# Keys and values of the next batch made in the unused columns of the score tiles

## The chip, the cores and the metric

The kernel runs on one core of a Trainium2 chip. The metric is device time in microseconds (us), the median of three runs. The names of the engines are those of the profile: PE (TensorE, with its weight loads as PEld), DVE (VectorE), ACT (ScalarE), POOL (GpSimd) and SP (SyncE, which issues the DMAs here).

## What is computed

An attention over pooled keys, and behind it a feed-forward layer with a SoLU activation and a layer norm. Four batches of 12288 queries, 768 keys each, width 128, hidden width 1024:

```python
kv_pool = kv.reshape(B, H // r, r, W // r, r, C).mean(axis=(2, 4))
kv_flat = kv_pool.reshape(B, -1, C) @ w_sr
k = v = kv_flat
s = scale * (q @ k.transpose(0, 2, 1))
a = np.exp(s - s.max(-1, keepdims=True))
a /= a.sum(-1, keepdims=True) + 1e-09
x = (a @ v).reshape(B * S, C)
h = x @ w_in
e = np.exp(h - np.max(h, axis=-1, keepdims=True))
solu = h * (e / (np.sum(e, axis=-1, keepdims=True) + 1e-09))
ln = (solu - mean(solu)) / np.sqrt(var(solu) + 1e-06) * g_ln
out = ln @ w_out
```

## The kernel before, in words

The rows of all batches are cut into 384 tiles of 128 queries, 96 tiles to a batch; four tiles are a group. One loop runs over 384 slots. A slot works on several tiles at once, each in another stage, so the engines are a pipeline, and the order in which the loop writes its calls is the order in which each engine works: nothing is rescheduled (`tc.manual_schedule`). In slot t:

- PE makes the scores of tile t+1 (`scores_pe`, L386): six matmuls into a PSUM tile `s` of two banks, 2 x 512 float32 columns, of which 2 x 384 are used.
- DVE takes the maximum of a score row (`nm`, L402, for tile t at the head of slot t), ACT the exponent in place (L403) and its rounded high part (`phl`, L407), DVE the low part (the score split, L415). DMA transposes both (`pT`).
- PE multiplies the transposed weights with the values of the batch (`values`, L453): 18 matmuls a group into one PSUM bank `xa`, spread over four slots, the quarters of the group. `values_out` (ACT, `xh`, L459) and `values_split` (DVE, `xl`, L464) read it when a group is done.
- PE makes the hidden row of tile t-9 (`hidden_pe`, `h`, L505, six matmuls), DVE the scaled maximum of tile t-10 (`junkd`, L513), ACT its exponent (`e`, L529), and in the slot behind it DVE the product `u` (L543), ACT the sum of squares (`junk`, L603), POOL the two float16 parts of `u` (`uhl`, L560 and L566). DMA transposes them (`uT`).
- PE makes the output of tile t-13 (`final_pe`, `o`, L631, 24 matmuls), which DVE scales (`ob`, L674).

The score tiles `s` and the hidden tiles `h` share three PSUM buffers in turn (`ps_r`). So the hidden product of slot t starts when DVE's split of tile t has read its score tile, and the scores of slot t start when `u` of tile t-11 has read its hidden tile.

On DVE a slot runs: hidden maximum, score split, (in one slot of four the reciprocal `rz`, L487, and half of `ob`; in another the other half), score maximum of the next tile, `u`, (in one slot of four `xl`). On ACT: `e`, (in one slot of four `xh`; in another a small `rz` and the rounding of the next queries `qh`), score exponent, `phl`, `junk`, then the next `e`.

Keys and values of batch b+1 are made beside batch b by a table `PLAN` of slots (counted within batch b). Its sum over the 16 pooled rows lies in `ka`. PE multiplies it with the weights (`kv_k_pe`, L235, in slots 69 and 73, one half of 384 keys each) and ACT copies the product to `ks` (L238). From `ks` come the rounded parts: `kv_kh` (ACT, L241, slots 72 and 76), `kv_sq` (ACT, a sum of squares, L260, slots 75 and 77), `kv_kl` and `kv_kc` (POOL). In slots 85 and 89 PE transposes `ks` (`kv_v_pe`, L286, three blocks a half) and ACT copies the result with a scale to `vf` (L291). Both kinds of product go to the bank of `xa`, in the one slot of a group in which the values of the last group are read and those of the next not yet begun; in these four slots the values of the first quarter (three matmuls instead of four) are written behind the hidden and the final product (`late`, `with_keys`). ACT's copy stands behind `e` of its slot. All this happens three times (batch 0's own keys are made ahead of the loop): in slots 69 to 91, 165 to 187 and 261 to 283.

Of the kernel before, what the change touches and what calls it, by code (L numbers as in the profile page):

```python
# [17 lines left out]
AF = mybir.ActivationFunctionType  # L18
# [4 lines left out]
B = 4  # L23
# [6 lines left out]
TPB = NTOK // P  # L30
WARM = 14
NT = B * TPB
GT = 4
GPB = TPB // GT
NG = NT // GT
# [9 lines left out]
LAV = 2  # L45
# [32 lines left out]
def kernel(  # L78
# [15 lines left out]
    nc = tc.nc  # L94
# [47 lines left out]
    state = {}  # L142
# [17 lines left out]
    def half_of(name, b, half):  # L160
        return state[name, b][:, half * 384 : half * 384 + 384]
# [67 lines left out]
    def kv_psum(b, name):  # L229
        pool, tag = (ps_x, "x") if b or name == "pv_0_0" else (ps_o, "o")  # L230
        return pool.tile([P, 512], F32, tag=tag, name=name)

    def kv_k_pe(b, half):
        state["pk", half] = kv_psum(b, f"pk_{b}_{half}")
        nc.tensor.matmul(state["pk", half][:, :384], w_sr16, half_of("ka", b, half), start=True, stop=True)  # L235

    def kv_k_out(b, half):
        nc.scalar.copy(half_of("ks", b, half), state.pop(("pk", half))[:, :384])  # L238

    def kv_kh(b, half):  # L240
        nc.scalar.copy(half_of("kh", b, half), half_of("ks", b, half))  # L241
# [125 lines left out]
    def scores_pe(t):  # L367
        g, j = divmod(t, GT)
        b = t // TPB
        qh, ql = state["q", g]  # L370
        qt = state["qf", g // QL].bitcast(BF16).rearrange("p (n two) -> p n two", two=2)[:, :, 1]
        kh, kl, kc = (state[n, b] for n in ("kh", "kl", "kc"))
        ts = slice(j * P, (j + 1) * P)
        s = ps_r.tile([P, 2, 512], F32, tag="r", name=f"s_{t}")
        if t in PY:
            py = s[:, 0, 384:385]
            for half in range(2):
                nc.tensor.matmul(
                    py, onesm, state["kss", PY[t]][:, half : half + 1], start=half == 0, stop=half == 1
                )  # L380
            state["py", PY[t]] = py
        row = [(n, half, *x) for n, x in enumerate(((ql, kc), (qh, kh), (qt, kl))) for half in range(2)]
        if t == 0:
            row = sorted(row[2:4] + row[:2] + row[4:], key=lambda x: x[1])
        for n, half, lh, rh in row:
            nc.tensor.matmul(  # L386
                s[:, half, :384],
                lh[:, ts],
                rh[:, half * 384 : (half + 1) * 384],
                start=n == (t == 0),  # L390
                stop=n == 2,
            )
        state["s", t] = s[:, :, :384]

    def scores_exp(t, between=()):

        g, j = divmod(t, GT)
        if j == 0:
            state["z", g] = tiny.tile([P, GT], F32, tag="z", name=f"z_{g}", bufs=4)
        s = state["s", t]  # L400
        nm = tiny.tile([P, 1], F32, tag="nm", name=f"nm_{t}", bufs=3)
        nc.vector.tensor_reduce(nm, s, axis=AX.XY, op=ALU.max, negate=True)  # L402
        nc.scalar.activation(s, s, AF.Exp, bias=nm, accum_out=state["z", g][:, j : j + 1])  # L403
        for f in between:
            f()
        phl = dmt.tile([P, 2, 2, 384], F16, tag="phl", name=f"phl_{t}", bufs=4)
        nc.scalar.mul(phl[:, 0], s, SC)  # L407
        state["phl", t] = phl
# [15 lines left out]
        )  # L424


    def with_keys(g):


        b, ti = divmod(GT * g + GT - 1 + LAV, TPB)  # L430
        return g > 1 and b + 1 < B and ti in WITH_PE

    def values(g, qtr, part):
        share = {0: [0, 6, 6, 6], 1: [0, 6, 6, 6]}.get(g, [4, 5, 5, 4])
        if with_keys(g):
            share = [3, 5, 5, 5]
        s0 = sum(share[:qtr])
        s1 = s0 + share[qtr]
        if s0 == s1:
            return  # L440
        cut = s0 + (s0 > 0)
        s0, s1 = ((s0, cut), (cut, s1))[part]
        b = g * GT // TPB
        if s0 == 0 and s1:
            state["xa", g] = ps_x.tile([P, 512], F32, tag="x", name=f"xa_{g}")
        if s0 == s1:
            return
        xa, pT = state["xa", g], state["pT", g]
        vh, vl = state["vh", b], state["vl", b]
        seq = [(a, c, v) for c in range(NKC) for (a, v) in ((0, vh), (1, vh), (0, vl))]  # L450
        for n in range(s0, s1):
            a, c, v = seq[n]
            nc.tensor.matmul(  # L453
                xa, v[:, c, :], pT[:, :, a * NKC + c, :], start=n == 0, stop=n == len(seq) - 1
            )
# [239 lines left out]
    ident = const.tile([P, P], F32, name="ident")  # L695
# [7 lines left out]
    w_sr16 = const.tile([P, P], F32, name="w_sr16")  # L703
# [139 lines left out]
    def w_low():  # L843
# [14 lines left out]


    PLAN = [  # L860
        (69, 0, kv_k_pe, kv_k_out), (73, 1, kv_k_pe, kv_k_out),
        (72, 0, kv_kh), (76, 1, kv_kh),
        (73, 0, kv_kl), (77, 1, kv_kl), (78, 0, kv_kc), (82, 1, kv_kc),
        (75, 0, kv_sq), (77, 1, kv_sq),
        (80, 0, kv_bound), (81, 1, kv_bound), (84, 2, kv_bound),
        (85, 0, kv_v_pe, kv_v_out), (87, 0, kv_v_high), (88, 0, kv_v_low),
        (89, 1, kv_v_pe, kv_v_out), (90, 1, kv_v_high), (91, 1, kv_v_low),
    ]
    WITH_PE = {slot for slot, _, *fs in PLAN if len(fs) > 1}


    def at(t, fn, *args):
        if 0 <= t < NT:
            fn(t, *args)
# [13 lines left out]
    for b in range(1, B):  # L888
        for k, fs in kv_plan(b):
            plan.setdefault((b - 1) * TPB + k, []).append(fs)  # L890
    scores_pe(0)
    for slot in range(NT):
        i = slot - LH
        av, qtr = divmod(slot - LAV - GT + 1, GT)
        tb, ti = divmod(slot, TPB)
# [3 lines left out]
        todo = plan.pop(slot, [])  # L899
# [11 lines left out]
        if 0 <= av < NG:  # L911
            values(av, qtr, 0)
        at(slot + 1, scores_pe)
        at_soon(slot - NORM, values_norm)
        at_last(slot - FSC, final_scale)
# [10 lines left out]
            hidden_var(i - 1)  # L926
        for f in fill.get(slot, []):
            f()
        pairs = [st for st in todo if len(st) > 1 and st[0].func is not kv_add]
        for st in pairs:  # L930
            st[0]()
        late = 0 <= av < NG and qtr == 0 and with_keys(av)
        if 0 <= av < NG and not late:
            values(av, qtr, 1)
        for st in pairs:
            for f in st[1:]:
# [12 lines left out]
        at_last(slot - LO, final_half, 0)  # L949
        if slot < NT - 1:  # L950
            at(slot - LO, final_pe)
        if late:
            values(av, qtr, 1)
        at(i - 1, hidden_turn)
        at_last(slot - LO - 1, final_out)
        at_last(slot - XSP, values_out)
# [18 lines left out]
    def tail_values(g):  # L975
# [5 lines left out]
        h=hidden_pe, M=hidden_max, E=hidden_exp, U=hidden_u, J=hidden_var, hi=hidden_high,  # L981
# [49 lines left out]
```

## Time and profile before

| what | value |
|---|---|
| median of 3 runs | 1853.36 us (1851.58 to 1855.24) |
| profiled execution, first to last instruction (span) | 1847.1 us |
| median of the runs less the span | 6.3 us |
| busy PE, DVE, ACT, POOL | 99%, 97%, 95%, 87% |
| granted TensorE clock | 0.9 or more of full speed in all 40 slices of the page; 1.000 as the mean |
| DMA engines, mean busy share by slice | 0.8 to 0.9 and more |

The page gives the profiled execution its span and no other time; the 6.3 us by which the timed median is longer are taken to lie around it. A busy PE counts each matmul with its modelled tail, and these overlap: what a matmul costs is the time from its start to the next one's. The same holds, by about a tenth of a microsecond, for DVE and ACT.

### The profile page before, as it was taken

The page shows a single profiled execution, that of the slowest core. Times are in us where ns is not written, and L with a number is a line of the kernel's source. Part 1 is how long each engine was busy: PE and PEld are TensorE (multiplying, and loading weights), DVE is VectorE, ACT ScalarE, POOL GpSimd, SP SyncE. Part 2 cuts the span into 40 slices and gives each one's busy share as a digit, 9 for nine tenths or more (in the row PEclk, how much of TensorE's full clock was granted, in tenths as well). Part 3 has the DMA queues.
Part 4 walks back from the last instruction along what each step waited for, and adds up shares of the span by engine and source line. Part 5 has one row for each costly group of instructions (what it writes and reads, how often), then busy time and mean ns, then how long its engine had stood idle before and what let it go on. Part 6 is the DMA issues. An engine that isn't in the chain of part 4 may idle for free.

```text
span 1847.1 us, 43152 instructions
## 1 busy us (share of the span) xinstructions
PE 1821.1 (99%) x15717; PEld 1179.2 (64%) x15718; DVE 1784.9 (97%) x2729; ACT 1752.8 (95%) x3148; POOL 1613.8 (87%) x1392
## 2 busy tenths in 40 slices
PE   8999999999999999999999999999999999999999
PEld 4566666666666666666666666666666666666666
DVE  7999999999999999999999999999999999999998
ACT  6999999999999999999999999999999999999998
POOL 3899889899998999989988899989888888888887
PEclk9999999999999999999999999999999999999999
DMA  8999999999999999999999999999999999999998
GB/s 300 208 238 233 229 245 234 236 240 245 232 234 240 244 238 241 235 233 238 235 233 234 247 241 241 238 236 231 227 217 230 233 228 223 230 227 231 224 223 179
DMA packets 1473253, 431.80 MB, mean 234 GB/s; under 512 B 1400977, under 2 KB 1454353, under 8 KB 1472785
## 3 DMA queue, kind: packets, MB, share of 16 engines
q1 hardware_dynamic: 1472752, 428.98, 114.1%
q8 instruction: 124, 2.03, 0.5%
q14 instruction: 89, 0.72, 0.1%
q10 hardware_dynamic: 288, 0.07, 0.0%
HBM read 52.50 MB, written 25.17 MB: 42 GB/s over the span
## 4 chain that ended last, share of the span: by engine, by line
PE 63%; DVE 13%; ACT 7%; POOL 7%; issue 7%; DMA 3%; DVEq 0%; POOLq 0%; ACTq 0%
PE o L631 19%; PE h L505 18%; PE xa L453 13%; PE s L386 13%; DVE junkd L513 3%; DVE nm L402 3%; POOL uhl L566 3%; DVE phl L415 2%; ACT e L529 2%; DMA pT<-phl 2%; ACT junk L603 2%; POOL uhl L560 2%; ACT phl L407 2%; DVE u L543 1%; DVE ob L674 1%
## 5 line engine op out<-in xcount | busy, mean ns | idle before, releaser
L566 POOL TENSOR_TENSOR uhl<-u,uhl 128x1024 f16<-128x1024 f32 x382 | 815.1, 2134 | 31.7 <-ACT uhl L558 0.2
L631 PEld LDWEIGHTS <-uT 128*128 128x128 f16 x9072 | 537.1, 98 | 91.9 <-DMA uT<-uhl 7.0
L631 PE MATMUL o<-wch,uT 128*128 128x128 f16 x6048 | 568.0, 219 | 1.3 <-DMA uT<-uhl 1.3
L631 PE MATMUL o<-wcl,uT 128*128 128x128 f16 x3024 | 525.9, 219 | 0.0
L560 POOL TENSOR_SCALAR uhl<-u 128x1024 f16<-128x1024 f32 x377 | 393.5, 1044 | 136.2 <-DVE u L543 131.1
L543 DVE SCALAR_TENSOR_TENSOR u<-h,rz,e 128x1024 f32<-128x1024 f32 x384 | 491.2, 1279 | 16.0 <-ACT e L529 3.6
L513 DVE TENSOR_SCALAR_CACHE_REDUCE junkd<-h,rz 128x1024 bf16<-128x1024 f32 x384 | 491.5, 1280 | 1.4 <-PE h L505 1.0
L529 ACT ACTIVATE e<-h,nm,rz 128x1024 f32<-128x1024 f32 x384 | 459.0, 1195 | 1.0 <-DVE junkd L513 1.0
L603 ACT ACTIVATE junk<-u,su 128x1024 bf16<-128x1024 f32 x384 | 437.8, 1140 | 0.2 <-DVE u L543 0.2
L402 DVE TENSOR_REDUCE nm<-s 128x1 f32<-128x768 f32 x384 | 365.7, 952 | 23.3 <-PE s L386 20.8
L453 PE MATMUL xa<-pT,vh 128*128 128x512 f16 x1152 | 373.5, 379 | 6.6 <-DMA pT<-phl 4.0
L403 ACT ACTIVATE s<-s,nm 128x768 f32<-128x768 f32 x384 | 335.9, 875 | 41.9 <-DVE nm L402 37.1
L415 DVE SCALAR_TENSOR_TENSOR phl<-s,phl 128x768 f16<-128x768 f32 x384 | 366.3, 954 | 4.5 <-ACT phl L407 4.3
L407 ACT ACTIVATE phl<-s 128x768 f16<-128x768 f32 x384 | 311.0, 810 | 11.7
L505 PEld LDWEIGHTS <-xh 128*128 128x128 f16 x1536 | 144.8, 97 | 191.7 <-issue 26.7
L386 PE MATMUL s<-kh,qh 128*128 128x384 f32 x768 | 248.0, 404 | 0.1
L505 PE MATMUL h<-w_in_h,xh 128*128 128x512 f16 x768 | 228.2, 379 | 3.5 <-DVE rz L487 2.4
L505 PE MATMUL h<-w_in_h,xl 128*128 128x512 f16 x768 | 228.4, 379 | 0.0
L505 PE MATMUL h<-w_in_l,xh 128*128 128x512 f16 x768 | 228.3, 379 | 0.0
L453 PE MATMUL xa<-pT,vl 128*128 128x512 f16 x576 | 218.3, 379 | 0.0
L386 PE MATMUL s<-kc,ql 128*128 128x384 bf16 x768 | 187.8, 326 | 7.4 <-DVE phl L415 4.4
L386 PE MATMUL s<-kl,qf 128*128 128x384 bf16 x768 | 192.2, 332 | 0.1
(127 smaller groups left out, 1707.2 us busy)
## 6 DMA issues: line engine op xcount, KB each, us to landing
kv<-in_kv_dram SPq DMA_DIRECT2D x64, 384.0 KB, 4.3
qf<-in_q_dram SPq DMA_DIRECT2D x96, 256.0 KB, 3.3
out_dram<-ob SPq DMA_DIRECT2D x95, 256.0 KB, 2.8
pT<-phl SPq DMA_TRANSPOSE x384, 3.8
uT<-uhl SPq DMA_TRANSPOSE x378, 4.4
raw_in<-in_moe_w_in_dram SPq DMA_DIRECT2D x1, 1024.0 KB, 5.4
raw_out<-in_moe_w_out_dram SPq DMA_DIRECT2D x1, 1024.0 KB, 8.6
out_dram<-ob SPq DMA_DIRECT2D x1, 192.0 KB, 2.0
```

Of the source, the lines that this page charges most:

```text
L386: nc.tensor.matmul(s[:, half, :384], lh[:, ts], rh[:, half * 384 : (half + 1) * 384], start=n == (t == 0), stop=n == 2,)
L402: nc.vector.tensor_reduce(nm, s, axis=AX.XY, op=ALU.max, negate=True)
L415: nc.vector.scalar_tensor_tensor(phl[:, 1], state.pop(("s", t)), SC, phl[:, 0], op0=ALU.mult, op1=ALU.subtract)
L453: nc.tensor.matmul(xa, v[:, c, :], pT[:, :, a * NKC + c, :], start=n == 0, stop=n == len(seq) - 1)
L505: nc.tensor.matmul(h[:, hs], lh[:, ts], rh[:, hs], start=n == 0, stop=n == 2)
L513: nc.vector.tensor_scalar(junk, state["h", t], state["rz", g][1][:, j : j + 1], None, op0=ALU.mult, op1=ALU.min, accum_out=nm,)
L529: nc.scalar.activation(e, state["h", t], AF.Exp, bias=nm, scale=state["rz", g][0][:, js], accum_out=state["z2", g][:, js],)
L543: nc.vector.scalar_tensor_tensor(u, state.pop(("h", t)), state["rz", g][2][:, j : j + 1], state.pop(("e", t)), op0=ALU.mult, op1=ALU.mult, ...
L560: nc.gpsimd.tensor_scalar(uhl[:, 0, :], u, 1.0, 1.0, op0=ALU.mult, op1=ALU.mult)
L566: nc.gpsimd.tensor_tensor(uhl[:, 1, :], u, uhl[:, 0, :], op=ALU.subtract)
L603: nc.scalar.activation(junk, u, AF.Square, scale=-float(DFF), bias=su, accum_out=state["v3", g][:, j : j + 1],)
L631: nc.tensor.matmul(po[:, ts], uT[:, a * NFC + c, :], w[:, c, :], start=start, stop=stop)
```

## The change

The products of the next batch's keys, and their transposes, no longer go to the bank of `xa`. They go to the columns 384 to 511 of the two banks of the score tile that the slot has just made (`state["room", "s"]`), 2 x 128 columns at a time. So the two halves of 384 become three thirds of 256: keys in slots 69, 70 and 74, transposes in slots 85, 86 and 89. The values of every group are four, five, five and four matmuls a quarter again and stand ahead of the hidden product in all slots.

```diff
-    def kv_k_pe(b, half):
-        state["pk", half] = kv_psum(b, f"pk_{b}_{half}")
-        nc.tensor.matmul(state["pk", half][:, :384], w_sr16, half_of("ka", b, half), start=True, stop=True)
-
-    def kv_k_out(b, half):
-        nc.scalar.copy(half_of("ks", b, half), state.pop(("pk", half))[:, :384])
+    def two_of(name, b, n):
+        return state[name, b][:, n * 256 : n * 256 + 256].rearrange("p (h k) -> p h k", h=2)
+
+    def kv_k_pe(b, n):
+        for h in range(2):
+            nc.tensor.matmul(
+                state["room", "s"][:, h], w_sr16, two_of("ka", b, n)[:, h], start=True, stop=True
+            )
+
+    def kv_k_out(b, n):
+        nc.scalar.copy(two_of("ks", b, n), state["room", "s"])
+
+    def kv_v2_pe(b, n):
+        for h in range(2):
+            nc.tensor.transpose(state["room", "s"][:, h], two_of("ks", b, n)[:, h], ident)
+
+    def kv_v2_out(b, n):
+        nc.scalar.activation(
+            two_of("vf", b, n), state["room", "s"], AF.Copy, scale=state["bb", b][:, 5:6]
+        )
...
         state["s", t] = s[:, :, :384]
+        state["room", "s"] = s[:, :, 384:]
...
         share = {0: [0, 6, 6, 6], 1: [0, 6, 6, 6]}.get(g, [4, 5, 5, 4])
-        if with_keys(g):
-            share = [3, 5, 5, 5]
...
-        (69, 0, kv_k_pe, kv_k_out), (73, 1, kv_k_pe, kv_k_out),
+        (69, 0, kv_k_pe, kv_k_out), (70, 1, kv_k_pe, kv_k_out), (74, 2, kv_k_pe, kv_k_out),
...
-        (85, 0, kv_v_pe, kv_v_out), (87, 0, kv_v_high), (88, 0, kv_v_low),
-        (89, 1, kv_v_pe, kv_v_out), (90, 1, kv_v_high), (91, 1, kv_v_low),
+        (85, 0, kv_v2_pe, kv_v2_out), (86, 1, kv_v2_pe, kv_v2_out),
+        (87, 0, kv_v_high), (88, 0, kv_v_low), (89, 2, kv_v2_pe, kv_v2_out),
+        (90, 1, kv_v_high), (91, 1, kv_v_low),
...
-        late = 0 <= av < NG and qtr == 0 and with_keys(av)
-        if 0 <= av < NG and not late:
+        if 0 <= av < NG:
             values(av, qtr, 1)
...
-        if late:
-            values(av, qtr, 1)
```

Three places in the built order, all around slots 69 and 70; the number behind a name is the tile or the group, and the brackets name the engine or queue whose semaphore the instruction waits for. On DVE, from the hidden maximum of tile 59 (slot 69) to the score maximum of tile 71 (slot 71), before:

```order
L513 TENSOR_SCALAR junkd_59_4826,nm2_59_4825<-h_59_4760,rz_14_4525 128x1024 [waits DVE_49,PE_49]
L415 SCALAR_TENSOR_TENSOR phl_69_4803<-s_69_4738,phl_69_4803 128x768 [waits DMAHW5_49,Activation_49]
L487 RECIPROCAL rz_15_4817<-zz_15_4816 128x8 [waits Pool_49]
L674 SCALAR_TENSOR_TENSOR ob_13_0_4767<-o_13_4556,swi_100,f2_13_4672 128x256 [waits PE_49]
L402 TENSOR_REDUCE nm_70_4882<-s_70_4809 128x1 [waits PE_49]
L543 SCALAR_TENSOR_TENSOR u_59_4887,su_59_4888<-h_59_4760,rz_14_4525,e_59_4828 128x1024 [waits Activation_49]
L513 TENSOR_SCALAR junkd_60_4905,nm2_60_4904<-h_60_4839,rz_15_4817 128x1024 [waits DVE_49,PE_49]
L415 SCALAR_TENSOR_TENSOR phl_70_4885<-s_70_4809,phl_70_4885 128x768 [waits DMAHW7_49,Activation_49]
L402 TENSOR_REDUCE nm_71_4948<-s_71_4891 128x1 [waits PE_49]
```

and with the change:

```order
L520 TENSOR_SCALAR junkd_59_4826,nm2_59_4825<-h_59_4760,rz_14_4525 128x1024 [waits DVE_49,PE_49]
L430 SCALAR_TENSOR_TENSOR phl_69_4803<-s_69_4738,phl_69_4803 128x768 [waits DMAHW5_49,Activation_49]
L494 RECIPROCAL rz_15_4817<-zz_15_4816 128x8 [waits Pool_49]
L681 SCALAR_TENSOR_TENSOR ob_13_0_4767<-o_13_4556,swi_100,f2_13_4672 128x256 [waits PE_49]
L417 TENSOR_REDUCE nm_70_4883<-s_70_4809 128x1 [waits Activation_49]
L550 SCALAR_TENSOR_TENSOR u_59_4888,su_59_4889<-h_59_4760,rz_14_4525,e_59_4828 128x1024
L520 TENSOR_SCALAR junkd_60_4906,nm2_60_4905<-h_60_4844,rz_15_4817 128x1024 [waits DVE_49,PE_49]
L430 SCALAR_TENSOR_TENSOR phl_70_4886<-s_70_4809,phl_70_4886 128x768 [waits DMAHW7_49,Activation_49]
L417 TENSOR_REDUCE nm_71_4952<-s_71_4892 128x1 [waits Activation_49]
```

The instructions stand in the same order. What moved is a wait: the two score maxima, which waited for PE, now wait for ACT, and `u` behind them has no wait of its own left. On ACT, from `e` of tile 59 to the exponent of tile 71, with the change:

```order
L536 ACTIVATE e_59_4828,z2_14_4547<-h_59_4760,nm2_59_4825,rz_14_4525 128x1024 [waits DVE_49]
L243 COPY ks_1_653<-s_70_4809 128x256 [waits PE_49]
L499 ACTIVATE rz_15_4817<-rz_15_4817,bb_0_125 128x4 [waits DVE_49]
L368 CAST qh_18_4880<-qf_18_4433 128x512 [waits DMAHW7_49,Pool_49]
L418 ACTIVATE s_70_4809,z_17_4728<-s_70_4809,nm_70_4883 128x2x384 [waits DVE_49]
L422 ACTIVATE phl_70_4886<-s_70_4809 128x768 [waits DMAHW7_49,Activation_49]
L610 ACTIVATE junk_59_4903,v3_14_4548<-u_59_4888,su_59_4889 128x1024 [waits DVE_49]
L536 ACTIVATE e_60_4908,z2_15_4842<-h_60_4844,nm2_60_4905,rz_15_4817 128x1024 [waits DVE_49]
L243 COPY ks_1_653<-s_71_4892 128x256 [waits PE_49]
L418 ACTIVATE s_71_4892,z_17_4728<-s_71_4892,nm_71_4952 128x2x384 [waits DVE_49]
```

Before, the first copy stood at the same place (of 384 columns, from `pk`), and the second was not there: the copies stand behind `e` of their slot and ahead of the exponent of the tile whose banks they read. On PE, behind the scores of tile 70 in slot 69, with the change:

```order
L238 MATMUL s_70_4809<-ka_1_567,w_sr16_94 128x128 x2
L460 LDWEIGHTS vh_0_126 [waits DMAHW5_49,DMAHW7_49,DMAHW2_49,DMAHW0_49]
L460 MATMUL xa_16_4832<-pT_16_4465,vh_0_126 128x512 [waits DVE_49]
L460 LDWEIGHTS vh_0_126
L460 MATMUL xa_16_4832<-pT_16_4465,vh_0_126 128x512
L460 LDWEIGHTS vl_0_127
L460 MATMUL xa_16_4832<-pT_16_4465,vl_0_127 128x512
L460 LDWEIGHTS vh_0_126
L460 MATMUL xa_16_4832<-pT_16_4465,vh_0_126 128x512
L512 LDWEIGHTS xh_15_4795 [waits DVE_49,Activation_49]
L512 MATMUL h_60_4844<-w_in_h_95,xh_15_4795 128x512 [waits PE_49]
```

Before, one key product of 384 columns into `pk`, which waited for DVE (the reader of `xa`), stood there, directly ahead of the hidden product `h_60`; the four value matmuls have come in between.

## Rows read from the trace of the kernel before

**Rows 1.** The page: busy time, share of the span, instructions of each engine.

```profile
PE 1821.1 (99%) x15717; PEld 1179.2 (64%) x15718; DVE 1784.9 (97%) x2729; ACT 1752.8 (95%) x3148; POOL 1613.8 (87%) x1392
```

**Rows 2.** Chain that ended last, 1230 to 1300 us: start, length in us, what.

```profile
1237.28 0.87 DVE phl L415
...
1241.95 1.02 PE s L386 x6
1242.97 0.86 PE xa L453 x4
1243.84 1.29 PE h L505 x6
1245.13 1.34 PE o L631 x24
```

**Rows 3.** Timeline of PE, slots 261 to 270: start, length, what, [idle before, releaser].

```profile
1236.36 0.49 PE L386 MATMUL s<-kc,ql 128*128 128x384 bf16 x2
...
1237.38 0.81 PE L235 MATMUL pk<-ka,w_sr 128*128 128x384 f32 x2
1238.30 0.59 PE L505 MATMUL h<-w_in_h,xh 128*128 128x512 f16 x2
...
1256.77 0.81 PE L235 MATMUL pk<-ka,w_sr 128*128 128x384 f32 x2
1257.43 0.59 PE L505 MATMUL h<-w_in_h,xh 128*128 128x512 f16 x2
...
1279.64 0.49 PE L386 MATMUL s<-kc,ql 128*128 128x384 bf16 x2
```

**Rows 4.** Timeline of PE, slots 277 to 285.

```profile
1312.22 0.49 PE L386 MATMUL s<-kc,ql 128*128 128x384 bf16 x2
...
1314.15 0.59 PE L505 MATMUL h<-w_in_h,xh 128*128 128x512 f16 x2 [0.42 <-DVE rz L487]
...
1350.75 0.49 PE L386 MATMUL s<-kc,ql 128*128 128x384 bf16 x2
```

**Rows 5.** Timeline of DVE, slots 261 and 262.

```profile
1238.06 0.20 DVE L487 RECIPROCAL rz<-zz 128x8 f32<-128x8 f32 x1
...
1238.52 0.95 DVE L402 TENSOR_REDUCE nm<-s 128x1 f32<-128x768 f32 x1
1239.39 1.28 DVE L543 SCALAR_TENSOR_TENSOR u<-h,rz,e 128x1024 f32<-128x1024 f32 x1
...
1240.59 1.28 DVE L513 TENSOR_SCALAR_CACHE_REDUCE junkd<-h,rz 128x1024 bf16<-128x1024 f32 x1
...
1241.79 0.96 DVE L415 SCALAR_TENSOR_TENSOR phl<-s,phl 128x768 f16<-128x768 f32 x1
1243.01 0.96 DVE L402 TENSOR_REDUCE nm<-s 128x1 f32<-128x768 f32 x1 [0.26 <-PE s L386]
```

**Rows 6.** Timeline of ACT, slots 261 and 262.

```profile
1237.31 1.20 ACT L529 ACTIVATE e<-h,nm,rz 128x1024 f32<-128x1024 f32 x1
...
1238.51 0.47 ACT L238 COPY ks<-pk 128x384 f32<-128x384 f32 x1
1238.87 0.30 ACT L492 ACTIVATE rz<-rz,bb 128x4 f32<-128x4 f32 x1
...
1239.58 0.88 ACT L403 ACTIVATE s<-s,nm 128x768 f32<-128x768 f32 x1
...
1242.44 1.19 ACT L529 ACTIVATE e<-h,nm,rz 128x1024 f32<-128x1024 f32 x1
```

**Rows 7.** Groups of instructions by line: busy us, mean ns | idle before, releaser.

```profile
L464 DVE SCALAR_TENSOR_TENSOR xl<-xa,xh 128x512 f16<-128x512 f32 x96 | 66.0, 687 | 0.0
...
L291 ACT ACTIVATE vf<-pv,bb 128x384 f32<-128x384 f32 x8 | 4.5, 574 | 0.0
```

**Rows 8.** Timeline of POOL, slots 76 to 82: the first and last of 28 pieces without idle.

```profile
365.21 1.04 POOL L560 TENSOR_SCALAR uhl<-u 128x1024 f16<-128x1024 f32 x1 [0.40 <-DVE u L543]
...
398.47 1.27 POOL L362 TENSOR_TENSOR ql<-qf,qh 128x512 bf16<-128x512 f32 x1
```

More of the change, by code (lines that the diff above doesn't have):

```diff
@@ L424, in scores_turn @@
         )
-    def with_keys(g):
-        b, ti = divmod(GT * g + GT - 1 + LAV, TPB)
-        return g > 1 and b + 1 < B and ti in WITH_PE
     def values(g, qtr, part):
         share = {0: [0, 6, 6, 6], 1: [0, 6, 6, 6]}.get(g, [4, 5, 5, 4])
-        if with_keys(g):
-            share = [3, 5, 5, 5]
         s0 = sum(share[:qtr])
@@ L865 @@
         (80, 0, kv_bound), (81, 1, kv_bound), (84, 2, kv_bound),
-        (85, 0, kv_v_pe, kv_v_out), (87, 0, kv_v_high), (88, 0, kv_v_low),
-        (89, 1, kv_v_pe, kv_v_out), (90, 1, kv_v_high), (91, 1, kv_v_low),
+        (85, 0, kv_v2_pe, kv_v2_out), (86, 1, kv_v2_pe, kv_v2_out),
+        (87, 0, kv_v_high), (88, 0, kv_v_low), (89, 2, kv_v2_pe, kv_v2_out),
+        (90, 1, kv_v_high), (91, 1, kv_v_low),
     ]
-    WITH_PE = {slot for slot, _, *fs in PLAN if len(fs) > 1}
     def at(t, fn, *args):
@@ L928 @@
             f()
-        pairs = [st for st in todo if len(st) > 1 and st[0].func is not kv_add]
+        pairs = [st for st in todo if len(st) > 1]
         for st in pairs:
             st[0]()
-        late = 0 <= av < NG and qtr == 0 and with_keys(av)
-        if 0 <= av < NG and not late:
+        if 0 <= av < NG:
             values(av, qtr, 1)
```

## The prediction, made before the changed kernel was run

> **What bounds the kernel now.** The busy shares come first [rows 1], and they only say that four engines are nearly full: PE 99%, DVE 97%, ACT 95%, POOL 87%. So I price a slot on each engine, from start to start. Three views give that: the chain that ended last, whose pieces are the times that an engine was really held [rows 2], and the timelines of DVE and ACT in slots 261 and 262 [rows 5, 6].
>
> PE: 1.02 us for the scores, 1.29 for the hidden product, 1.34 for the output, 0.86 for four value matmuls, 0.215 each [rows 2]. A group of four slots has 18 of these: 4 x 3.65 + 18 x 0.215 = 18.47 us. A slot with five is 4.73, one with three 4.30.
>
> DVE: hidden maximum 1.20 (1240.59 to 1241.79), split 0.87 [rows 2, 5], score maximum 0.87 (1238.52 to 1239.39), `u` 1.20, that is 4.14 a slot; in one slot of four 0.46 for `rz` and a half of `ob` (1238.06 to 1238.52), in another about 0.35 for the other half, and `xl`, 0.69 long [rows 7], some 0.6 from start to start. A group is at least 18.0 us. So PE is the bound, and DVE has only 0.5 us a group to spare.
>
> ACT: from `e` to what stands behind it 1.20; from the score exponent to the next `e`, over `phl` and `junk`, 2.86 (1239.58 to 1242.44) [rows 6].
>
> The other side of the loop is that PE needs DVE: the hidden product reads a buffer that the split frees. In slot 261 it starts 1.11 us behind the split's start (1237.19, which is 0.87 ahead of `rz`; 1238.30) [rows 3, 5], and the chain goes through DVE there (`phl` at 1237.28) [rows 2]. In an ordinary slot of that phase PE is ready at 1.02 + 0.86 = 1.88 and the split lets it at 0.83 + 1.11 = 1.94: a later DVE is a later PE.
>
> **The change, part by part.** The third batch of keys (slots 261 to 283) is the cleanest to count on; the other two repeat it.
>
> Work of PE. In slot 265 a half of the keys holds PE 0.66 us (1256.77 to 1257.43) [rows 3], two make 1.3. The new six products have as many columns, 768. Their price in pieces of 128 isn't in the trace of this loop; bounds are nothing extra, and a tenth of a microsecond for each of the four added; I take 1.34 in all, 0.45 a third. The transposes stay six. Value matmuls stay 18 a group. So PE's work stays as it was within 0.05 us a batch.
>
> Waits removed. In slot 261 the hidden product follows the key product by 0.92 (1237.38 to 1238.30) [rows 3] and not 0.66: 0.26 lost, because three value matmuls that could have filled the time stand behind. Slots 261 to 269 take 43.28 (1236.36 to 1279.64) [rows 3]; two groups, a slot of 4.73 and 1.3 for keys make 42.97, so 0.3 is lost. Slots 277 to 284 take 38.53 (1312.22 to 1350.75), two groups and 0.65 of transposes make 37.6, so 0.9 is lost, and its largest piece has DVE as the one waited for (1314.15, 0.42 shown) [rows 4]. The change puts four value matmuls, 0.86 us, into these places, and all of it could go: 1.2 us a batch, 3.6 in all.
>
> The wait added. The built order shows it: the score maximum of the tile whose banks hold the products waits for ACT's copy, and no longer for PE. Six times a batch. The copy stands behind `e`, and `e` waits for the hidden maximum of the same slot. Behind the score maximum on DVE stand `u` (for which POOL, `junk` and PE's next scores wait), the next hidden maximum (for which `e` waits) and the next split (for which the next hidden product waits).
>
> Price of a copy: 0.47 us for 384 columns, and 0.36 until the next instruction of ACT starts [rows 6]. For 256 it is between two thirds (0.31) and the whole (0.47) until it is done; I take 0.34, and 0.04 more to DVE's start. The scaled copy of the transposes is 0.57 for 384 [rows 7], so 0.38 to 0.57; I take 0.45.
>
> Slot 261, counted from its first score matmul at 1236.36: `e` starts at 0.95, the copy at 2.15, the maximum at 2.15 + 0.38 = 2.53 and not at 2.16 [rows 5, 6]. The score exponent starts when it is done, 0.98 behind it, at 3.5 and not 3.22, so the next `e` is at 3.5 + 2.86 = 6.36 and not 6.08. PE's slot, with a third of the keys and five value matmuls, is 4.73 + 0.45 = 5.18.
>
> Slot 262, from 5.18 on: `e` at 1.18, the copy at 2.38, the maximum at 2.76. Today it starts at 1.22 (1243.01 less 1241.79) [rows 5]. DVE could have started at 1.5, as its hidden maximum and split are done then, so it idles 1.26: from hidden maximum to hidden maximum this slot takes 5.4 and not 4.14.
>
> The same sum goes on with the slots behind, each instruction at the later of what stands ahead of it and what it waits for. DVE's steps are 4.98, 5.41, 4.59, 5.09, where PE asks for 5.18, 5.18, 4.73, 4.30. In slot 265 the hidden maximum starts 0.17 behind the first score matmul (in slot 261 today it is 0.37 ahead: 1237.19 less 1.20, against 1236.36). So the split is done only 2.47 into the slot, PE wants the hidden product at 1.88, and waits 0.59. The third copy (slot 266) costs DVE another 1.26, and ACT's squares and rounding in slots 267 to 269, 0.3 to 0.4 each by the copy of the same size, keep it from catching up: waits of 0.12, 0.46 and 0.59 there. By slot 270 the rhythm is the old one. The waits sum to 1.94 over slots 261 to 269, with 42.95 of work: 44.89, against 43.28: **+1.6**.
>
> For the transposes the copies are longer and PE's extra work is less (0.22 a third), so there is less to hide behind. By the same sum PE waits 0.5 in slot 278 (its next scores for `u`), 0.25 in 279, 0.1 in 280, 0.5 in 281, 0.25 in 282: 1.6 and 37.55 of work make 39.15, against 38.53: **+0.6**.
>
> In the first two batches POOL runs 28 pieces without a gap from a `u` in slot 76 to the queries `ql` on which the scores of tile 84 wait [rows 8]. It starts with that `u`, 1.75 later than today by the same sum, so there the 1.6 becomes 1.75: 0.3 in all.
>
> Sum: 3 x (1.6 + 0.6) + 0.3 = 6.9, say 7.0. On the profiled span that is 1854.1. The runs' median is 6.3 above the span, which the change doesn't touch: 1860.4 us, **0.38% slower**.
>
> [...]
>
> **Rivals.**
>
> *The wait is absorbed.* DVE has 0.5 us a group to spare and PE's key work gives it 0.9 more in slots 261 and 262. If the copies start earlier than I count (ACT ahead of PE by a microsecond), the maximum is late by less than that, PE never waits and the 1.2 a batch is won: about -3.5, 1849.9, faster. It decides in slot 265: the hidden maximum has to start 0.4 or more ahead of the first score matmul. Against it: the copy can't pass `e`, and `e` can't pass the hidden maximum, in every slot.
>
> *Half of it.* The copies are at the short end and the steps of ACT overlap more than I count; the waits come to some 2 a batch in place of 3.5: +2 to +4, about 1856.5.
>
> *It spreads.* `u` late by 1.75 makes POOL, the transposes `uT` and the next groups late, in stretches where the DMA engines are at 0.9 and more. A microsecond more in each batch and each half: +11, 1864.5. For it: POOL has no gap over seven slots [rows 8]. Against: in the third batch nothing waits for POOL.
>
> *The change does nothing* is excluded by the order: waits and places differ.
>
> **How the numbers follow.** Forecast 0.70, half of it 0.13, absorbed 0.10, spreading 0.07. The runs of this kernel spread by 0.1% either way, so about 0.2% (3.7 us) is what a measurement can tell from no change: below 1849.7 is faster, above 1857.1 slower. Faster: half of the absorbed case and a little, 0.06. Same: the other half, half of the half case, a little of the forecast, 0.15. Slower: 0.79. The forecast's own range is 1857 to 1863.5, from the copies' bounds. To hold 8 in 10 the range goes down into the half case and up to the spreading one: 1854 to 1864.
>
> **What would show it.** In the changed profile DVE's idle time ahead of the score maximum is put down to ACT's copy, 18 times, some 5 us a batch, the largest near 1.3 in slots 70, 74 and 86 of a batch. The hidden product behind a key or transpose product no longer waits, and hidden products three to eight slots later do, for DVE, 0.5 to 0.6 at most. Slots 261 to 269 take about 44.9, slots 277 to 284 about 39.15. If the maximum doesn't wait for ACT, or waits while PE's slots keep to 4.73 and 4.30, the forecast is wrong by its main term. If copies of 256 columns take far from 0.34 and 0.45, its size is wrong.

## The result, and the profile after

The changed kernel takes 1862.93 us (median of four runs, 1861.03 to 1864.58), the kernel before 1852.78 on the same chip: a ratio of 1.0056 (95% interval 1.0042 to 1.0070), 10.15 us slower. The prediction was +7.0 us, 1860.4, range 1854 to 1864.

The page of the changed kernel (answers to [rows 1]):

```profile
PE 1828.8 (98%) x15742; PEld 1182.1 (64%) x15742; DVE 1783.4 (96%) x2729; ACT 1755.3 (94%) x3154; POOL 1613.2 (87%) x1392
```

The shares tell as little as before; the count of PE's matmuls, 15742 where before has 15718 (one record is missing in [rows 1]), will matter further down. Timeline of PE, slots 261 to 270 and 277 to 285 (answers to [rows 3, 4]); the rows of `s<-kc,ql` are the first of each slot:

```profile
1245.84 0.49 PE L400 MATMUL s<-kc,ql 128*128 128x384 bf16 x2
1246.86 0.61 PE L238 MATMUL s<-ka,w_sr 128*128 128x128 f32 x4
1248.17 0.59 PE L512 MATMUL h<-w_in_h,xh 128*128 128x512 f16 x2
...
1251.02 0.49 PE L400 MATMUL s<-kc,ql 128*128 128x384 bf16 x2
...
1265.39 0.49 PE L400 MATMUL s<-kc,ql 128*128 128x384 bf16 x2
1267.96 0.59 PE L512 MATMUL h<-w_in_h,xh 128*128 128x512 f16 x2 [0.54 <-DVE rz L494]
...
1282.92 0.60 PE L512 MATMUL h<-w_in_h,xh 128*128 128x512 f16 x2 [0.23 <-DVE phl L430]
...
1288.13 0.59 PE L512 MATMUL h<-w_in_h,xh 128*128 128x512 f16 x2 [0.53 <-DVE rz L494]
...
1290.98 0.49 PE L400 MATMUL s<-kc,ql 128*128 128x384 bf16 x2
...
1323.58 0.49 PE L400 MATMUL s<-kc,ql 128*128 128x384 bf16 x2
...
1334.06 0.48 PE L400 MATMUL s<-kc,ql 128*128 128x384 bf16 x2 [0.40 <-DVE u L550]
...
1345.91 0.59 PE L512 MATMUL h<-w_in_h,xh 128*128 128x512 f16 x2 [0.30 <-DVE rz L494]
...
1362.78 0.33 PE L400 MATMUL s<-kc,ql 128*128 128x384 bf16 x1
```

Slots 261 to 269 take 45.14 us (1245.84 to 1290.98; 43.28 before, 44.89 predicted), slots 277 to 284 take 39.20 (1323.58 to 1362.78; 38.53 before, 39.15 predicted). The hidden product behind the keys no longer waits (1248.17, 2.33 us into its slot, where 1.02 for the scores, 0.45 for the keys and 0.86 for four values end). The ones four and eight slots later do (1267.96 and 1288.13). The idle time shown is less than the loss, since it counts from the modelled end of the matmul ahead. In slot 268 the releaser shown is DVE's split (`phl`), as predicted. In slots 265 and 269 it is `rz`, the short instruction directly behind the split. The hidden product doesn't read `rz`; it needs the buffer that the split has read, and it starts 1.10 us behind the split's start, as in [rows 3, 5]. Which of the two ends the wait there can't be told from these times; both come late with the split.

Timeline of DVE, slots 261 and 262 (answers to [rows 5]), and its split of slot 265:

```profile
1247.63 0.43 DVE L681 SCALAR_TENSOR_TENSOR ob<-o,swi,f 128x256 f32<-128x256 f32 x1
1248.36 0.96 DVE L417 TENSOR_REDUCE nm<-s 128x1 f32<-128x768 f32 x1 [0.30 <-ACT ks L243]
...
1251.64 0.95 DVE L430 SCALAR_TENSOR_TENSOR phl<-s,phl 128x768 f16<-128x768 f32 x1
1253.80 0.96 DVE L417 TENSOR_REDUCE nm<-s 128x1 f32<-128x768 f32 x1 [1.20 <-ACT ks L243]
...
1266.86 0.95 DVE L430 SCALAR_TENSOR_TENSOR phl<-s,phl 128x768 f16<-128x768 f32 x1
```

Timeline of ACT, slot 262 (answers to [rows 6]):

```profile
1252.22 1.19 ACT L536 ACTIVATE e<-h,nm,rz 128x1024 f32<-128x1024 f32 x1
...
1253.40 0.36 ACT L243 COPY ks<-s 128x256 f32<-128x256 f32 x1
1254.79 0.88 ACT L418 ACTIVATE s<-s,nm 128x768 f32<-128x768 f32 x1 [1.02 <-DVE nm L417]
```

One reads a circle in them: `e`, then the copy, then DVE's maximum (1253.80, as the copy is done), then ACT's exponent, which waited 1.02 for it. The maxima start 2.52 and 2.78 into their slots; 2.53 and 2.76 were predicted. The copies take 0.36 us for keys and 0.47 for transposes (means of nine; 0.34 and 0.45 were taken). The waits of DVE in the changed kernel, and of PE (us in total, times, the longest):

```profile
DVE nm L417 <- ACT ks L243: 8.1, 9, 1.2
DVE nm L417 <- ACT vf L250: 6.3, 9, 1.3
```

```profile
PE h L512 <- DVE rz L494: 4.8, 10, 0.7
...
PE s L400 <- POOL ql L376: 2.6, 6, 0.6
PE s L400 <- DVE u L550: 2.5, 6, 0.7
```

The same three waits in the kernel before:

```profile
PE h L505 <- DVE rz L487: 2.4, 7, 0.7
PE s L386 <- POOL ql L362: 1.5, 4, 0.5
PE s L386 <- DVE u L543: 1.3, 3, 0.7
```

So DVE waits 18 times for a copy, 14.4 us, 4.8 a batch. The table shows where the time goes, by stretches of PE's timeline in one execution of each kernel, from first score matmul to first score matmul; the ratio is that of the medians. "Keys" are slots 69 to 92, 165 to 188 and 261 to 285, "loads" slots 13 to 68, 93 to 164 and 189 to 260, in which the next batch's keys come in, and "last" is from the scores of the last tile to the end of DVE's last instruction. The expectations below count the loads one or two slots earlier (938.6 us for before) and the last stretch from one tile earlier (49.3).

| kernel | keys | loads | last | ratio to before (95%) |
|---|---|---|---|---|
| before | 349.42 | 938.20 | 44.55 | |
| changed | 357.57 | 941.29 | 45.70 | 1.0056 (1.0042 to 1.0070) |
| copies behind the exponent (e1) | 348.81 | 941.14 | 45.84 | 1.0023 (1.0013 to 1.0034) |
| copies made twice (e2) | 366.01 | 938.45 | 45.96 | 1.0100 (1.0085 to 1.0114) |
| keys only (e3) | 355.50 | 939.65 | 45.91 | 1.0042 (1.0026 to 1.0058) |
| transposes only (e4) | 351.87 | 936.46 | 44.55 | 1.0004 (0.9994 to 1.0013) |
| other slots (e5) | 354.59 | 938.92 | 45.69 | 1.0042 (1.0029 to 1.0055) |
| copies on DVE (e6) | 350.12 | 938.95 | 45.43 | 1.0013 (1.0004 to 1.0021) |
| before again (e7) | 349.77 | 937.04 | 44.55 | 0.9995 (0.9987 to 1.0004) |
| transposes only, copies behind (e10) | 347.41 | 941.42 | 44.55 | 0.9999 (0.9990 to 1.0008) |
| before, 48 instructions more (e11) | 351.00 | 944.03 | 45.60 | 1.0048 (1.0029 to 1.0067) |
| e1, 208 more (e12) | 348.93 | 942.68 | 44.54 | 1.0036 (1.0020 to 1.0051) |
| before, 48 more, start not delayed (e13) | 350.04 | 942.10 | 45.62 | 1.0051 (1.0038 to 1.0065) |
| before, 256 more (e14) | 349.47 | 936.72 | 44.55 | 1.0002 (0.9993 to 1.0010) |

The changed kernel loses 8.15 in the keys (2.7, 2.7 and 2.8 a batch), 1.15 in the last stretch, which the change doesn't touch, and 3.1 in the loads of this one execution. Slots 286 to 381 take the same in both kernels, 444.4 and 444.5.

### The profile page after: what moved, and what is told of

Read it like the earlier page. It is cut to its first block, busy times and chain, and to the rows that moved or that the text cites. A ratio compares the mean times of both kernels' runs of the same rounds, so it can differ in the third digit from the quotient of the medians.

```text
span 1860.6 us, 43207 instructions
## 1 busy us (share of the span) xinstructions
PE 1828.8 (98%) x15742; PEld 1182.1 (64%) x15742; DVE 1783.4 (96%) x2729; ACT 1755.3 (94%) x3154; POOL 1613.2 (87%) x1392
## 3 DMA queue, kind: packets, MB, share of 16 engines
q8 instruction: 124, 2.03, 0.5%
## 4 chain that ended last, share of the span: by engine, by line
PE 57%; DVE 12%; POOL 10%; ACT 9%; issue 8%; DMA 4%; DVEq 0%; POOLq 0%; ACTq 0%
PE o L638 16%; PE h L512 16%; PE s L400 12%; PE xa L460 12%; POOL uhl L573 4%; DVE nm L417 3%; DVE junkd L520 3%; ACT e L536 3%; ACT junk L610 3%; DMA pT<-phl 2%; POOL uhl L567 2%; DVE phl L430 2%; ACT phl L422 2%; DVE u L550 1%; POOL ka L227 1%
```

## The experiments

The theory: DVE's score maximum waits for ACT's copy. Rivals: the products in smaller pieces and the order of the values cost PE the time; or it spreads over DMA and POOL. In each diff the lines are the edit against the changed kernel, where nothing else is said.

**e1: the copies behind the score exponent.**

```diff
-        (69, 0, kv_k_pe, kv_k_out), (70, 1, kv_k_pe, kv_k_out), (74, 2, kv_k_pe, kv_k_out),
+        (69, 0, kv_k_pe), (70, 1, kv_k_pe), (74, 2, kv_k_pe),
+        (70, 0, kv_k_out), (71, 1, kv_k_out), (75, 2, kv_k_out),
...
-    BETWEEN = (kv_kh, kv_sq)
+    BETWEEN = (kv_k_out, kv_v2_out, kv_kh, kv_sq)
...
```

> The changed kernel, with one thing moved: ACT's six copies a batch stand no longer behind e of the slot that made the products, but one slot later, between the score exponent and phl of the same tile. PE, DVE, POOL and the DMAs have the same instructions in the same order; ACT has the same ones, six a batch at another place. The score maximum then waits for PE again, and only the split, which waits for phl anyway, comes behind the copy. Theory (the score maximum's wait for ACT's copy): by the sum of the prediction slots 261 to 269 take 43.1 us (changed kernel 45.14, before 43.28) and slots 277 to 284 37.55 (39.20, 38.53); DVE's idle time ahead of the score maximum is no longer put down to the copies. Against before that is -0.2 and -1.0 a batch, -3.5 in all: some 1849.5 us. Rival one (the smaller pieces on PE and the order of the values cost it): the same PE work, so slots 261 to 269 stay at 45 and the time at 1863. Rival two (DMA and POOL in the stretches between): the slots named fall by less than half and the time stays above 1857.

Measured: 1852.91 us beside 1849.24, ratio 1.0023. Timeline of ACT, and of DVE, slot 262:

```profile
1246.25 0.88 ACT L418 ACTIVATE s<-s,nm 128x768 f32<-128x768 f32 x1 [0.26 <-DVE nm L417]
1247.27 0.37 ACT L243 COPY ks<-s 128x256 f32<-128x256 f32 x1
1247.54 0.82 ACT L422 ACTIVATE phl<-s 128x768 f16<-128x768 f32 x1
```

```profile
1245.26 0.96 DVE L417 TENSOR_REDUCE nm<-s 128x1 f32<-128x768 f32 x1 [0.45 <-PE s L238]
```

The maximum starts 1.66 into its slot (first score matmul at 1243.60) and not 2.78, and no longer waits for ACT. The keys stretches fall by 8.76, below before. The two slot sums miss the expectation a little: 43.57 us (43.1) and 37.73 (37.55), and slot 285 takes 5.04 in place of 4.73. With the same PE instructions as the changed kernel, this excludes the smaller pieces and the order of the values. The total is off by more: -3.5 was expected and +3.7 came, while the keys give -0.6. In the execution profiled the rest lies in the loads (+2.9) and in the last stretch (+1.3).

**e2: each copy twice** (the loop over the copies runs twice).

```diff
-            for f in st[1:]:
+            for f in st[1:] * 2:
```

> The changed kernel with each of the 18 copies made twice, one behind the other on ACT; nothing is left out. Theory: the score maximum comes later by one more copy, 0.34 us for keys and 0.45 for transposes. By the same sum slots 261 to 269 take 45.9 (+1.0 by the sum) and slots 277 to 284 40.5 (+1.35), so +2.4 a batch and +7 in all, 1870 us; the idle time of DVE ahead of the score maximum grows from some 14.4 us in all by 0.3 to 0.45 at each of 18 places, that is by 6 to 7. Rival one (pieces and order on PE): no change, 1863. Rival two (spread over DMA and POOL): a change, but less than half of it in the slots named. If ACT itself were the bound, the time would rise by what ACT does more: 18 copies of 0.23 to 0.33, 5 us.

Measured: 1867.38, ratio 1.0100. The keys stretches rise by 8.44 over the changed kernel; slots 261 to 269 take 46.38 (45.9 was expected) and 277 to 284 take 40.75 (40.5). The waits of DVE:

```profile
DVE nm L417 <- ACT ks L243: 11.8, 9, 1.6
DVE nm L417 <- ACT vf L250: 10.9, 9, 1.8
```

8.3 us more of DVE's waiting make 8.4 us more of time; ACT's own work grew by 5 by the expectation's count. The dose goes with the wait.

**e3 and e4: one half of the change each.** Only the named products go to the score tiles; the others, their slots and `late` are as before.

> Half of the change: the key products go to the free columns of the score tiles (slots 69, 70, 74), the transposes to the bank of xa as before (two halves in slots 85 and 89, with three values in the quarter). Theory: slots 261 to 269 take what they take with the whole change, 45.1 us (43.28 before), slots 277 to 284 what they take before, 38.5. In the first two batches POOL adds 0.2 to 0.5 each. Sum against before: 3 x 1.9 and 0.3 to 1: +6 to +6.5, some 1859 us. Rival one (pieces on PE): the same sign but by PE's own work and not by DVE's idle time. Rival two (spread): the two halves of the change don't add up, as the rest comes from stretches between.

> The other half of the change: the transposes of the keys go to the free columns of the score tiles (slots 85, 86, 89), the key products to the bank of xa as before (two halves in slots 69 and 73). Theory: slots 261 to 269 take 43.3 us as before, slots 277 to 284 39.2 with 0.2 to 0.3 behind them (38.53 before). Sum against before: 3 x 0.9, +2.6, some 1855.4 us. With the half that has the keys it should make the whole difference of the two kernels, +8.5 by the slots and +10 by the medians, within 2 us.

Measured: 1857.64 (ratio 1.0042) and 1849.87 (1.0004). Slots 261 to 269 take 45.17 and 43.26, slots 277 to 284 take 38.54 and 39.22: each half carries its own stretch. In the keys they cost 6.08 and 2.45, together 8.53, the whole change 8.15. The totals are a miss for both: +8.4 for the first half, above its 6.08 and the +6 to +6.5 expected, and +0.6 for the second, below its 2.45; its loads were the shortest of all. Their sum, +9.0, is the whole change's 10.15 within the 2 us that were named.

**e5: the products only in slots 1 mod 4.**

```diff
...
+        (69, 0, kv_k_pe, kv_k_out), (73, 1, kv_k_pe, kv_k_out), (77, 2, kv_k_pe, kv_k_out),
+        (74, 0, kv_kh), (78, 1, kv_kh),
+        (75, 0, kv_kl), (79, 1, kv_kl), (79, 0, kv_kc), (82, 1, kv_kc),
+        (76, 0, kv_sq), (79, 1, kv_sq),
...
+        (85, 0, kv_v2_pe, kv_v2_out), (89, 1, kv_v2_pe, kv_v2_out), (93, 2, kv_v2_pe, kv_v2_out),
...
```

> The changed kernel with the six products at other slots: keys in slots 69, 73 and 77, transposes in slots 85, 89 and 93, the steps that need them later by as much. The copies still stand behind e and the score maximum still waits for them, but only in the slots in which rz and a half of ob stand ahead of the score maximum on DVE, so that it comes 0.4 to 0.5 us late in place of 1.3. Theory (the wait for the copy, sized by what DVE can still take up): by the sum the waits of PE are 0.6 us for keys and 0.8 for transposes a batch, where the changed kernel has 1.9 and 1.7; the time falls by some 2.2 a batch, to 0 to 2 us above before. If the number of waits counted and not their length (18 score maxima that wait for ACT, as now), or the pieces on PE, the time would stay 10 above before.

Measured: 1856.4, ratio 1.0042, a miss. In the third batch the sum holds: slots 261 to 285 take 118.86 (119.12 before, 121.93 changed), and 0.45 comes behind them. DVE waits 5.7 us for the copies in all, 0.4 at most, and not 14.4. The first two batches take 2.8 and 2.6 more than before, and the waits of PE and of POOL say why:

```profile
PE s L400 <- POOL ql L376: 5.9, 8, 1.0
```

```profile
POOL ka L227 <- PE s L238: 4.2, 2, 2.2
```

PE waits 3.3 longer than in the changed kernel for the queries `ql`, two thirds of it for those of tiles 80 and 84 of a batch. POOL makes these late because it stands still itself, 2.2 and 2.0 us. The sums `ka` of all batches share one buffer, so the first addition for the batch after next has to wait until PE has read the sum of the next one, and the last to read it, the third key product, moved from slot 74 to slot 77. The changed kernel has no such wait, and in the third batch there is no batch after next and no such addition. So the sum holds where only the copies' place differs; in the other two batches the move brought a wait of its own.

**e6: the copies on DVE**, directly ahead of the score maximum of the same tile.

```diff
-        nc.scalar.copy(two_of("ks", b, n), state["room", "s"])
+        nc.vector.tensor_copy(two_of("ks", b, n), state["room", "s"])
...
-    FRONT = (kv_bound,)
+    FRONT = (kv_bound, kv_k_out, kv_v2_out)
...
```

> The changed kernel with the six copies a batch made by DVE, directly ahead of the score maximum of the same tile. Nothing waits for ACT there any more; DVE has more work, 18 copies. A copy on DVE from a score bank is not in the trace; the score maximum over 768 columns takes 0.87, so 256 cost some 0.3, and not over 0.5. Theory: by the sum with 0.3, slots 261 to 269 take 43.2 us (45.14 in the changed kernel) and slots 277 to 284 37.7 (39.20): the time is that of the kernel with ACT's copies behind the exponent, within 1.5 us, some 0.2% above before. If DVE's load and not the wait made the loss (DVE has 0.5 us a group to spare), six times 0.3 a batch more would leave the time near the changed kernel, 8 or more above before.

Measured: 1851.59 beside 1849.14, ratio 1.0013. The keys fall by 7.45 against the changed kernel, the loss against before from 10.15 to 2.45. Groups of DVE:

```profile
L250 DVE TENSOR_SCALAR vf<-s,bb 128x256 f32<-128x256 f32 x9 | 4.2, 472 | 0.0
L243 DVE COPY ks<-s 128x256 f32<-128x256 f32 x9 | 3.8, 421 | 0.5
```

The copies cost 0.42 and 0.47 and not 0.3, 8.0 us of work on an engine at 96%, and the time still falls. The loss was the wait and not DVE's load.

**e7 and e10: before once more, and transposes alone with their copies behind the exponent** (e4 with e1's order).

> The kernel before, unchanged, as a control. Its slots 261 to 269 and 277 to 284 should repeat within 0.05 us (43.28 and 38.53). Open is what the stretches do in which the next batch's keys are loaded (slots 14 to 69, 93 to 165, 189 to 261): 938.6 us in the one trace of before, 936.4 to 941.2 in five traces of other kernels. If they differ by 2 us or more here, the differences there are scatter of the execution and belong to no kernel; if they repeat, they belong to the kernel. The time is that of before, ratio 1 within 0.1%.

> Keys as before (two halves in the bank of xa, slots 69 and 73); the transposes in the free columns of the score tiles, with ACT's copies behind the score exponent of the tile. Theory: slots 261 to 269 take 43.3 as before, slots 277 to 284 37.7 as in the kernel with all copies behind the exponent (38.53 before), so -0.6 a batch and no other difference in these stretches: -1.8 in all, some 0.1% faster than before, if the stretches in which the next batch's keys are loaded stay as they are. If what the kernel with all copies behind the exponent lost there (some 4 us against before, in stretches that the change doesn't touch) comes with the values' order or the free columns, this one loses it too: +2.

Measured: 1848.13 (0.9995) and 1848.44 (0.9999), beside 1849.14. Before repeats its keys within 0.4 and its last stretch exactly. The keys of e10 are 2.0 below before (0.7, 0.8 and 0.5 a batch), the only ones that are clearly so. Its loads took 941.42 in an execution of 1851.04, 2.6 above its median: the loads of a single trace can lie some microseconds off. Its time can't be told from before; it is faster than the changed kernel, and no version here is measurably faster than before.

The last stretch had by then taken two values. It was 44.55 where PE has 15718 matmuls, and 45.4 to 46.0 where it has 15742, whatever was done to the keys. Four runs test whether the count itself does that: the kernel before, or e1 (in e12), with one-column matmuls added ahead of the first key or in slots 1 and 2. In e11 and e12 four and eight of the 14 idle matmuls ahead of the first key are left out for them.

> The kernel before with 24 matmuls more on PE, each with its weight load, of one column: of the 14 idle matmuls that PE makes ahead of the first key, 10 stay and 28 of one column follow. Nothing behind them is changed; they fit into the 1.1 us in which PE waits for the first load there. Open in the two kernels is the last stretch, from the scores of the last tile to the end: 49.3 us in four kernels with 15718 matmuls (before twice, transposes only twice), 50.2 to 50.7 in six kernels with 15742, though the code there is the same. Theory: PE's instructions come in loads of 16 KB on a DMA queue of their own, and 48 instructions more move the loads earlier, into the last transposes, whose packets stand still for 1.7 us then (seen in the traces with 15742). Then this kernel, with 15742 matmuls and none of the change, takes 50.2 to 50.7 there, and some 1.2 us more in all. Rival: the last stretch belongs to the key products in the free columns or to what stands ahead of it; then it stays at 49.3.

> The kernel with ACT's copies behind the score exponent, with 104 matmuls of one column more (6 of the 14 idle matmuls ahead of the first key stay, 64 small ones follow, and 24 stand in each of slots 1 and 2). With the change's own 24 that makes 128 matmuls and 128 weight loads, 16 KB of instructions, so PE's loads fall at the end where they fall in before. Theory of the instruction loads: the last stretch is 49.3 us again (50.6 in the kernel with the copies behind, 15742 matmuls), and the slots of keys and transposes stay within 0.1 us. The head may be up to 2 us longer by PE's new work there. Rival: the last stretch stays at 50.6.

Measured: 1859.53 (ratio 1.0048) and 1857.22 (1.0036), beside 1850.92. The last stretch is 45.60 and 44.54, as the theory of the instruction loads has it. But e11 is 8.6 slower and not 1.2, most of it in the loads (944.03), and it starts later: the scores of slot 13 are at 70.05, where the two traces of before have 67.86 and 68.80. And e12 stays 6.3 above before, where e1 was 3.7 above it. The next diff is against the kernel before, whose `WARM` is 14.

```diff
-    for _ in range(WARM):
+    for _ in range(14):
         nc.tensor.matmul(idle, ones16, warm, start=True, stop=True)
+    for _ in range(24):
+        nc.tensor.matmul(idle[:, :1], ones16, warm[:, :1], start=True, stop=True)
```

> The kernel before with 24 one-column matmuls behind all of its 14 idle matmuls, so that the start is not delayed (0.03 us each, 0.75 in all, in a gap of 1.1). Open after the kernel with 48 more instructions and a start 1.4 us later: its load stretches (slots 14 to 69, 93 to 165, 189 to 261) took 944.1 us, 938.6 and 937.1 in the two traces of before. Theory: the place of PE's instruction loads decides there as at the end: the load stretches take 942 to 945, the last stretch 50.4 to 50.6, the time is 5 to 8 above before. Rival: the later start decided in the load stretches (other phase of the key loads against the transposes); then they take 936.5 to 939 here, the last stretch is still 50.4 to 50.6, and the time is some 1.2 above before.

> The kernel before with 128 one-column matmuls more, 256 instructions with their weight loads, 16 KB: 28 behind the 14 idle matmuls, 50 in each of slots 1 and 2. Each load of PE's instructions then falls where the one before it fell. Theory of the instruction loads: the last stretch is 49.3 us, the load stretches take 936.5 to 939 as in before, and the time is above before only by what the head is longer, 0 to 3 us. Rival: any more instructions, or a later start, cost time in the load stretches; then they take 942 or more.

Measured: 1858.40 (ratio 1.0051) and 1849.03 (1.0002), beside 1848.60. With 48 instructions more, and the scores of slot 13 at 67.84 as in before (67.86), the loads take 942.1 and the last stretch 45.62. With 256 more both are those of before. So the later start is not what made e11 slow. The profiled execution of e13 is 1854.53, 3.9 under its median, so its table row shows less than the whole. Timeline of ACT near the end, in e13 and in e14 (the same instruction):

```profile
1835.08 1.04 ACT L558 CAST uhl<-u 128x1024 f16<-128x1024 f32 x1 [0.96 <-DMA room<-uhl]
```

```profile
1828.81 1.05 ACT L558 CAST uhl<-u 128x1024 f16<-128x1024 f32 x1
```

And what the DMA engines moved in the 4 us around it, in 40 slices of 0.1 us, with the instruction queue; e13 from 1831.5 us, e14 from 1826.3:

```profile
GB/s 289 289 279 271 279 292 287 289 287 274 180 54 195 133 212 243 246 246 141 36 18 0 0 0 0 0 0 18 8 8 10 10 10 13 236 294 287 287 287 287
...
q8 instruction: 1, 0.02, 2.3%
```

```profile
GB/s 292 289 292 287 282 276 294 276 279 269 170 67 46 146 246 264 274 269 174 264 292 287 297 292 287 289 289 294 289 289 289 282 88 21 13 0 164 0 0 0
...
q8 instruction: 1, 0.02, 2.0%
```

In e14 the transposes go on at 290 GB/s and the load of instructions comes as a single slice of 164 when they are done. In e13 it falls among them, from 1832.8 us (the slice of 195, where e14 has 46): nothing moves for 0.6 us and then 8 to 18 GB/s for 0.7, and ACT waits 0.96 for the buffer that the transpose frees.

For the loads stretches the traces show less. From 68 to 1242 us, PE and its weight loads together wait for the transposes `pT` and `uT` 22.6 us in e13 and 28.4 in e11, but 16.5, 16.9 and 14.9 in before, before again and e14; so part of the added time shows as waits for the transposes. But of these waits 5.3 to 9.0 us lie within 4 us behind the start of an instruction load, in all five traces alike. That the place of the loads decides in these stretches, too, is not shown.

## Why the prediction was right, and what it missed

**What bounds the kernel, and the added wait.** The mechanism was right. e1 and e6 take the wait away in two ways and the keys fall by 8.8 and 7.5; e2 makes it longer and they rise by 8.4; e3 and e4 divide it as the two terms do. The wait is the one that the built order has: in the changed kernel the maximum, which reads other columns of the two banks, waits for the copy (1253.80, 1.20 us). No run has ACT and DVE read such a bank with no wait between them, so none shows what two engines in one bank would cost.

**The sizes.** +1.6 for slots 261 to 269 measured +1.86: the hidden products of slots 265 and 269 wait some 0.7 and not 0.59. +0.6 for slots 277 to 284 measured +0.67, and 0.26 came behind them in slot 285, which the sum left out. +0.3 in all through POOL is too small as a part of the first two batches, which take 2.7 each where 2.35 was said. Together 8.15 in place of 6.9. Two figures of the prediction's sum don't follow from its own terms: two groups, a slot of 4.73 and 1.34 for keys make 43.0 and not 42.95, and the waits that it names make 1.76 and not 1.94. With them slots 261 to 269 come to 44.8, a little further from the 45.14 measured.

**Waits removed, "all of it could go", 1.2 a batch.** This failed. With the wait for ACT away (e1) the keys are 0.2 a batch below before and not 1.2. Of the 0.9 for the transposes 0.8 came (37.73 against 38.53), but 0.3 of it went again in slot 285; of the 0.3 for the keys nothing came (43.57 against 43.28). Six copies on ACT still push `phl` and the split back (0.27 us each, 1247.27 to 1247.54), and the split is what the hidden product waits for. The rival in which the wait is absorbed, 1849.9, had this gain as its base; in e1, with no wait for ACT left, there is little to win.

**The base.** The 6.3 us "around the span" was 1.8 around it (a time of 1862.41 with a span of 1860.6; 1849.06 with 1847.3 for before again), and the other 4.5 are an execution quicker than that median. It was added on both sides, so the difference didn't suffer.

**What the prediction doesn't have.** Its sum has no term for the last stretch and the loads stretches. Of the 10.15, 8.15 lie in the keys and 1.15 in the last stretch, which leaves some 0.85 for the rest. So 2 of the 10.15 us were not foreseen, and that the time still lies in the range, near its upper end, is partly luck: that end was there for longer copies and for the spreading rival, and neither is what came. The last stretch is shown by e11 to e14 to follow the count of PE's instructions (45.60 and 45.62 us with 48 more than before, 44.54 and 44.55 with 256 more). For the loads of the changed kernel, which has 16, 32 and 48 more PE instructions behind its three key stretches, that is only argued: no run gave the changed kernel 208 more. The six kernels with the change's key products and 15742 matmuls take 335.1 to 340.1 us in slots 189 to 260, so one trace doesn't settle it. The same holds for e1's excess in the loads, and for why e12 is slow there, with other places of its instruction loads than before in all three batches.

## What to carry to other kernels

Free columns of a bank were not a free place here: a reader of them stands, in the built order, in line with the other engines that use the bank (18 waits of DVE for ACT, 14.4 us). So put it behind the reader that the critical engine waits for (e1, keys 8.8 us shorter), or on the engine that reads the bank next anyway (e6, 7.5 us shorter). Ask, for each wait that moves to another engine, what that engine does ahead of it; here `e`, 1.2 us, was more than the copy's price, 0.36 or 0.47. And before a difference of half a per cent is explained, see whether stretches with identical code have changed too: run the kernel with as many idle instructions added as the change adds.

## What was not expected of the hardware

PE's instructions are loaded during the run by DMA, 16 KB at a time, beside the transposes. The queue of these loads (their number, megabytes, and share of the DMA engines' time) in the kernel before, and in e14:

```profile
q8 instruction: 124, 2.03, 0.5%
```

```profile
q8 instruction: 125, 2.05, 0.5%
```

256 instructions more on PE are one load more (124 and 125). 2.03 MB in 124 loads make 16.4 KB a load, and the 15718 matmuls of before with as many weight loads make 254 instructions a load. The loads held up transposes beside them: in the trace of before a transpose's packet of 256 bytes takes 0.018 us in the median; 654 of 1.37 million take over 1.5, and all 654 run at the same time as a load, though the loads take only 140 us of the 1847. At the end of e13 ACT waits 0.96 us on such a transpose (1.04 in the changed kernel), and there the place of the load costs time: the last stretch takes 45.62 us, and 44.55 in e14. 48 instructions more (one-column matmuls, 0.03 us each by e12, which has 24 in 0.74, and in a gap, with their weight loads) made the kernel before 0.51% slower (interval 0.38 to 0.65), and 256 didn't (0.02%, -0.07 to 0.10). That is nearly as much as the whole change, 0.56%; how the part of it in the loads stretches arises stays open.
